# One row tile's normalisation moved to VectorE, key streams in another order, and an epsilon on VectorE, in a four-layer attention and MLP kernel

## The chip, the core and the metric

The kernel runs on one core of a Trainium2 chip. Its engines work side by side and wait for one another through semaphores: TensorE (matrix products, PE in the profile, with PEld for its weight loads), VectorE (DVE), ScalarE (ACT), GpSimd (POOL) and SyncE (SP), which here only issues DMAs. The metric is the device time of one execution in microseconds. Before the change it is 742.9 us, the median of three runs (742.76 to 743.25).

## The reference

An input x of 2048 rows (tokens) by 576 features passes through four layers, each with a residual: attention A, MLP B, then A and B again with the same weights.

```
x = x + A(layernorm(x));  x = x + B(layernorm(x));  x = x + A(layernorm(x));  x = x + B(layernorm(x))

A(x):  q, k, v = x @ wqkv            # 32 heads of 18 features
       phi(t) = where(t > 0, t + 1, exp(t)) + 1e-6
       kv = phi(k)^T v  per head;  z = sum over rows of phi(k)
       o = (phi(q) kv) / (phi(q) . z + 1e-6);   return o @ wo
B(x):  h = gelu(layernorm(x) @ w1 + b1)         # 4608 hidden features
       return h @ w2 + b2
```

The attention is linear: keys and values of all rows are first summed to one small matrix per head, and only then are the queries used. The denominators get 1e-6 added before the division.

## The kernel before

**Tiles.** The 2048 rows are 16 row tiles of 128 partitions, in four blocks of four tiles. x_sb holds x row by row, yT the normalised rows transposed (feature by row), as TensorE wants them. TensorE accumulates in eight PSUM banks: four single ones named one0 to one3 and two pairs, accA and accB. Program order on each engine is written out by hand: every engine executes in the order in which the code issues, and waits only for semaphores.

**Row tiling.** Most products use 64 of the 128 rows of TensorE's array, so that two streams, an upper (rows 0 to 63) and a lower one, run at the same time. A result is the sum of both halves, so both streams write the same PSUM bank in turn. Where one stream takes a bank over from the other, a relay stands between them: a tiny memset on GpSimd (`relay_by_pool`, line 306; in the MLP a copy on ScalarE) that waits for the last product of the one stream, and that the first product of the other stream waits for.

**The second attention's key stage.** `key_rows` (line 736) writes two lists of products, `upper` and `lower` (lines 813 to 818): `keys(t, hi)` are the key and value projections of tile t, nine products into two banks in turn of one0 to one2; `main(t, hi, k)` are the products of normalised rows with phi(k), into four banks k = 0 to 3 (accA, accB); `sides` are small products into one3. `row_streams` (line 261) merges the lists with a small planner: each product costs its columns at 2.4 per ns, a bank passes from stream to stream `PASS` = 0.5 us after its last product, and the stream that is ready first issues. Then it places relays: for each pass of a bank from product x to product y it looks for an existing relay between them that is due `RELAY` = 0.7 us before y, and else sets one as late as that allows. One relay may serve several banks, and then it waits for the last of its products. `key_half` (line 763) reads a finished bank: exponential and maximum with zero on ScalarE, sums on VectorE. That frees the bank for a later tile.

**The run-up to an MLP's first block.** After the key sums come the output products of the first block's tiles in the order 0, 2, 1, 3 (`wo_stage`), each followed on VectorE by the residual into x_sb and the statistics of the next layer's normalisation. `first` (line 1066) lists the four normalisations `Norm(t, "B", eng, transpose)`: `eng` says which engine normalises the row, `transpose` which one copies the transposed tile from PSUM to yT. Before, ScalarE normalises and copies the tiles 0 and 2, VectorE the tiles 1 and 3. GpSimd computes the reciprocal root (`rstd`, line 419: ln_u, ln_rstd, and ln_nmr where ScalarE normalises). Two query projections (`q_next`) go to one0 and one3, and ScalarE evicts them (an exponential and a maximum each). Then TensorE transposes tiles 0 and 2 (`transposed_halves`, line 469), and runs `q_batch` (line 671): 36 products for four query groups of the last block, into one2, one0, one1 and one3. The dictionary `between` names the number of products after which the transposes of tiles 1 and 3 come in. The MLP's first products (`m1_group`) follow.

**The denominators** of blocks 1 to 3 are computed within the MLP's first groups: `den_stage((1, 2, 3))` (line 971) sums them in one bank, ScalarE adds 1e-6 in place with an Identity activation whose bias is the constant tile den_eps, and VectorE takes the reciprocals. These go through DRAM to be spread over the partitions (`spread`), VectorE scales the queries with them, and `wo_pair` uses those.

Of the kernel before, what the change touches and what calls it, by code (L numbers as in the profile page):

```python
# [7 lines left out]
ACT = mybir.ActivationFunctionType  # L8
ALU = mybir.AluOpType
BF16 = mybir.dt.bfloat16  # L10
F32 = mybir.dt.float32
# [4 lines left out]
P = 128  # L16
NT = S // P
KD = 5
# [17 lines left out]
def build(tc, A_x, A_wqkv, A_wo, B_w1, B_b1, B_w2, B_b2, out, n_layers=4):  # L36
    nc = tc.nc
    with ExitStack() as ctx:
# [70 lines left out]
        quad_mask = const.tile([P, 4, P], BF16, name="quad_mask")  # L109
        zsel = const.tile([P, 6, H], BF16, name="zsel")  # L110
        eps_sel = const.tile([P, H], BF16, name="eps_sel")
        den_eps = const.tile([P, 1], F32, name="den_eps")
        last_two = const.tile([P, 2], F32, name="last_two")
        zk = const.tile([P, P], BF16, name="zk")

        def mask_batches():
            sel, fill = pool.affine_select, pool.memset
# [11 lines left out]
            def maskz_b():  # L129
                first = fill(zsel[:], 0.0)  # L130
                fill(eps_sel[:], 1e-6)
                fill(den_eps[:], 1e-6)
                fill(zk[:], 0.0)
                fill(last_two[:], 0.0)
                sel(out=last_two[:], in_=last_two[:], compare_op=ALU.not_equal, fill=1.0,
                    base=-126, pattern=[[-1, 2]], channel_multiplier=1)
                return first
# [123 lines left out]
        def row_streams(upper, lower, relay):  # L261


            ends, left, order, free, latest = [0.0, 0.0], [list(upper), list(lower)], [], {}, 0.0
            while left[0] or left[1]:
                ready = [max([ends[hi], latest] + [t + PASS for other, t in free.get(left[hi][0].bank, {}).items() if other != hi])
                         if left[hi] else 1e9 for hi in range(2)]
                hi = 0 if ready[0] <= ready[1] else 1
                op = left[hi].pop(0)
                op.at = latest = ready[hi]  # L270
                ends[hi] = op.at + max(op.n, 100) / 2400.0
                free.setdefault(op.bank, {})[hi] = ends[hi]
                order.append(op)

            user, passes = {}, []
            for i, op in enumerate(order):
                if op.bank in user and order[user[op.bank]].hi != op.hi:
                    passes.append((user[op.bank], i))
                user[op.bank] = i
            relays, needs = {}, {}  # L280
            for x, y in sorted(passes, key=lambda p: p[1]):
                found = [i for i in relays if x <= i < y and order[i].at + RELAY <= order[y].at]
                if not found:
                    found = [max([i for i in range(x, y) if order[i].at + RELAY <= order[y].at] or [x])]
                relays.setdefault(found[0], set()).add(x)
                needs.setdefault(y, set()).add(found[0])
            done, passed = {}, {}
            for i, op in enumerate(order):
                done[i] = op.emit()
                for r in needs.get(i, ()):  # L290
                    tc.add_manual_dep(done[i].ins, passed[r], SYNC, reason="row tiles take turns on a PSUM bank")
                if i in relays:
                    by = relay()
                    for x in relays[i]:
                        tc.add_manual_dep(by.ins, done[x].ins.name, SYNC, reason="row tiles take turns on a PSUM bank")
                    passed[i] = by.ins.name
                if op.then is not None:
                    op.then()


        PASS, RELAY = 0.5, 0.7

        def relay_by_act():
            return act.copy(out=relay_sb[:, 1:2], in_=relay_sb[:, 0:1])
# [257 lines left out]
        def layer_A(li, next_kind, begin, before_tile, before_keys, mid_tile, rows_ahead, after_tile, q_tiles, placed, mlp):  # L562
# [173 lines left out]
            def key_rows():  # L736
# [53 lines left out]
                def sides(t, hi):  # L790
                    rows, ops = HALVES[hi], []
                    for g in range(4):
                        def emit(g=g):
                            if "side" not in acc:
                                acc["side"] = one("side_ps", "one3")
                            first = "s" not in begun
                            begun.add("s")
                            return mm(acc["side"][:, 65 * g:65 * (g + 1)], pks[t][rows, GO[g]:GO[g] + P], ys[t][rows, 4 * P:D + 1],
                                      first, False, skip_group_check=True)
                        ops.append(RowOp("s", hi, 65, emit))  # L800
                    ops.append(RowOp("s", hi, 72, lambda: mm(acc["side"][0:VW, 264:336], vas[t][rows, :], pks[t][rows, V4:D],
                                                             False, False, skip_group_check=True)))
                    return ops

                def all_of(t, hi):
                    s = sides(t, hi)
                    return [main(t, hi, 0), main(t, hi, 1), main(t, hi, 2), s[0], main(t, hi, 3)] + s[1:]

                def some(t, hi, *ks):
                    return [main(t, hi, k) for k in ks]  # L810

                acc["main"] = [pair("rk_ps", "accA"), pair("rk_ps", "accB")]
                upper = some(0, 0, 0, 1) + keys(2, 0) + some(0, 0, 2, 3) + sides(0, 0) + keys(3, 0) + all_of(1, 0)
                lower = some(0, 1, 2, 3) + some(1, 1, 2, 3) + some(0, 1, 0, 1) + some(1, 1, 0, 1) + keys(2, 1) + sides(0, 1) + \
                    sides(1, 1) + keys(3, 1)
                for t in range(4, NT):
# [154 lines left out]
            def den_stage(cs):  # L971

                dp = one("den_ps", "one3" if cs[0] == 0 else None)
                for i, c in enumerate(cs):
                    to = dp[:, i * P:(i + 1) * P]
                    dens[c] = to
                    for g in range(G):
                        for j in range(TPC):
                            mm(to[32 * j:32 * (j + 1), :], zsel[:, g + (g == 4 and j // 2), :], q_tile(g, c, j),
                               g == 0 and i == 0, g == G - 1 and c > 0, skip_group_check=True)  # L980
                if cs[0] == 0:
                    for j in range(TPC):
                        mm(dp[32 * j:32 * (j + 1), 0:P], eps_sel[:], ident[:], False, True, skip_group_check=True)
                    return
                these = dp[:, 0:len(cs) * P]
                act.activation(out=these, in_=these, func=ACT.Identity, bias=den_eps[:, 0:1], scale=1.0)

            dens = {}

# [73 lines left out]
                    vec.tensor_tensor(out=rows, in0=acc[:, 0:HALF], in1=rows, op=ALU.add)  # L1063


            first = [Norm(t, "B", "act" if i < 2 else "dve", "act" if i < 2 else "dve") for i, t in enumerate((0, 2, 1, 3))]

            if not placed:
                most_sums()
# [56 lines left out]
            for tag in ("one0", "one3"):  # L1126
# [4 lines left out]
            first[0].transposed_halves(other[0])  # L1131
            first[1].transposed_halves(other[1])
            q_batch([units[:, i, :] for i in range(13, 17)], ("one2", "one0", "one1", "one3"),
                    {13: lambda: first[2].transposed_halves(other[0]), 25: lambda: first[3].transposed_halves(other[1])})
            one_turn.update(n=0, banks=4)
            warm_table(ACT.Gelu_apprx_tanh)
            assert not q_left
# [338 lines left out]
```

## Time and profile before

| what | value |
|---|---|
| median of three runs | 742.9 us |
| the profiled execution | 743.14 us |
| its span in the trace | 741.3 us |
| TensorE busy | 735.1 us, 99% |
| ScalarE busy | 302.7 us, 41% |
| VectorE busy | 270.7 us, 37% |
| GpSimd busy | 132.4 us, 18% |
| granted TensorE clock | 1.0 |

A row of the timeline has the start in us, the duration, the engine, the line of the code, the operation, output and inputs by name with their shape, the number of merged instructions (x), and in brackets the engine's idle time before it and what ended that. L229 is the helper through which nearly all TensorE products are issued, L53 the one of the other engines, so rows are told apart by their tiles: q_ps, k_ps, rk_ps (the four main banks of the key stage), side_ps, den_ps, wo_ps, hp_ps and h_ps (first MLP product), m_ps (second MLP product), tp (transposes), y_ring (normalised rows), units (queries and hidden features), pool_relay (relays). In merged groups of products the duration runs from the first start to the last end, and ends are modelled, so a short wait can be hidden under the end of the product before it. The chain that ended last is a list of start, duration and what ran.

### The profile page before, as it was taken

The numbers are of one execution on the slowest core, as the hardware profiler recorded it, in microseconds if no ns is written. First come the engines' busy times: TensorE is split into PE (matmuls) and PEld (weight loads), VectorE is DVE, ScalarE is ACT, GpSimd is POOL, SyncE is SP. The second block draws the span as 40 slices with busy tenths as digits, with TensorE's granted clock in tenths as the row PEclk, the third lists the DMA queues.
The fourth block names the chain that finished last, engine by engine and source line by source line (L and its number), as shares of the span: only waits on it lengthen the run. The fifth ranks groups of instructions, "written<-read, shape, count | busy, mean of one in ns | idle before, by whom it ended". The sixth has DMA issues, their size and how long they took to land.

```text
span 741.3 us, 21145 instructions
## 1 busy us (share of the span) xinstructions
PE 735.1 (99%) x9142; PEld 468.6 (63%) x9151; DVE 270.7 (37%) x688; ACT 302.7 (41%) x672; POOL 132.4 (18%) x404
## 2 busy tenths in 40 slices
PE   8999999999999999999999999999999999999998
PEld 4666556774576457646777655667646754774475
DVE  7868745434224403300376685552410060000000
ACT  5776743107601750374035676320373047106700
POOL 4541000322121202200223120031200130010010
PEclk9999999999999999999999999999999999999999
DMA  8945221112200220110024000202020002000000
GB/s 204 267 145 186 70 71 35 22 34 53 36 5 31 37 37 18 29 26 2 18 74 94 23 8 24 82 2 54 18 37 2 18 17 37 10 18 10 1 17 18
DMA packets 61315, 35.02 MB, mean 47 GB/s; under 512 B 37126, under 2 KB 61222, under 8 KB 61222
## 3 DMA queue, kind: packets, MB, share of 16 engines
q1 hardware_dynamic: 60470, 33.45, 17.8%
q8 instruction: 71, 1.16, 0.7%
q10 hardware_dynamic: 752, 0.23, 0.2%
q14 instruction: 22, 0.18, 0.1%
HBM read 21.70 MB, written 4.93 MB: 36 GB/s over the span
## 4 chain that ended last, share of the span: by engine, by line
PE 95%; DVE 2%; ACT 1%; DMA 1%; SPq 1%; issue 0%; POOL 0%; DVEq 0%; POOLq 0%
PE m_ps L229 38%; PE hp_ps L229 21%; PE h_ps L229 17%; PE k_ps L229 5%; PE q_ps L229 4%; PE rk_ps L229 4%; PE wo_ps L229 4%; ACT units L53 1%; PE side_ps L229 1%; SPq L53 1%; DMA x_sb<-in_A_x_dram 1%; DVE units L53 1%; ACT y_ring L53 1%; PE tp L465 0%; DVE ln_st L53 0%; PE den_ps L229 0%
## 5 line engine op out<-in xcount | busy, mean ns | idle before, releaser
L229 PEld LDWEIGHTS <-units 64*128 64x128 bf16 (+1 forms) x5070 | 260.9, 94 | 72.8 <-DVE units L53 0.8
L229 PE MATMUL m_ps<-w_sb,units 64*128 64x288 bf16 (+2 forms) x4432 | 283.7, 283 | 0.0
L229 PEld LDWEIGHTS <-w_sb 64*128 64x128 bf16 x2304 | 126.8, 94 | 132.3 <-issue 0.7
L229 PE MATMUL h_ps<-yT,w_sb 64*128 64x512 bf16 x1152 | 176.3, 376 | 0.0
L229 PE MATMUL hp_ps<-yT,w_sb 64*128 64x512 bf16 x1152 | 149.7, 376 | 0.0
L53 DVE TENSOR_TENSOR x_sb<-m_ps,xo 128x288 bf16<-128x288 f32 (+3 forms) x48 | 25.4, 554 | 336.5 <-PE m_ps L229 336.5
L53 ACT COPY relay_sb<-relay_sb 128x1 f32<-128x1 f32 x142 | 27.1, 191 | 260.0 <-PE m_ps L229 176.3
L53 ACT ACTIVATE units<-hp_ps,b1T 128x512 bf16<-128x512 f32 x144 | 91.2, 684 | 87.0 <-PE hp_ps L229 87.0
L53 POOL TENSOR_TENSOR xo<-x_sb,b_bc 128x576 f32<-128x576 bf16 x32 | 40.8, 1275 | 345.1 <-DVE x_sb L53 319.8
L53 ACT ACTIVATE units<-h_ps,b1T 128x512 bf16<-128x512 f32 x142 | 95.2, 687 | 0.1
L229 PE MATMUL k_ps<-wkv_sb,yT 64*128 64x288 bf16 (+3 forms) x432 | 61.0, 299 | 0.3 <-ACT yT L53 0.2
L229 PE MATMUL hp_ps<-yT,w_tail 64*128 64x512 bf16 x144 | 54.1, 376 | 0.0
L229 PE MATMUL h_ps<-yT,w_tail 64*128 64x512 bf16 x144 | 54.1, 376 | 0.0
L53 DVE BATCH_NORM_STATS2 ln_st<-x_sb 128x6 f32<-128x288 bf16 x128 | 51.6, 443 | 1.5 <-DMA x_sb<-in_A_x_dram 0.8
L229 PE MATMUL q_ps<-yT,wq_sb 64*128 64x512 bf16 (+2 forms) x273 | 42.0, 347 | 1.1 <-ACT units L53 0.7
L53 DVE STREAM_TRANSPOSE shared<-y_ring 128x640 bf16<-128x640 bf16 x40 | 32.7, 832 | 26.0 <-DMA yT<-shared 19.9
L229 PEld LDWEIGHTS <-yT 64*128 64x128 bf16 (+1 forms) x448 | 36.4, 95 | 8.7 <-ACT yT L53 0.7
L229 PE MATMUL wo_ps<-shared,units 64*128 64x288 bf16 (+1 forms) x480 | 38.1, 283 | 0.2 <-DVE units L53 0.2
L53 ACT ACTIVATE phi_e<-k_ps 128x288 bf16<-128x288 f32 x64 | 26.3, 413 | 29.5 <-PE k_ps L229 25.9
L53 POOL MEMSET pool_relay<- 128x1 f32 x152 | 17.0, 112 | 118.1 <-PE hp_ps L229 44.1
L53 POOL TENSOR_TENSOR ln_rstd<-ln_u,neg_half 128x1 f32<-128x1 f32 x64 | 36.5, 571 | 8.4 <-DVE ln_u L53 3.3
L229 PEld LDWEIGHTS <-w_tail 64*128 64x128 bf16 x288 | 27.1, 94 | 17.0
(112 smaller groups left out, 493.8 us busy)
## 6 DMA issues: line engine op xcount, KB each, us to landing
yT<-shared SPq DMA_DIRECT2D x160, 40.0 KB
w_sb<-in_B_w_dram SPq DMA_DIRECT2D x12, 432.0 KB
w_sb<-in_B_w_dram SPq DMA_DIRECT2D x9, 512.0 KB
yT<-rden_rows SPq DMA_DIRECT2D x24, 126.0 KB
y_rows<-y_ring SPq DMA_DIRECT2D x16, 144.0 KB
units<-y_rows SPq DMA_DIRECT2D x16, 144.0 KB
x_sb<-in_A_x_dram SPq DMA_DIRECT2D x15, 144.0 KB
out_dram<-x_sb SPq DMA_DIRECT2D x15, 144.0 KB
```

The lines of the kernel that those rows point to most:

```text
L53: inst = issue(*args, **kw)
L229: return pe(nc.tensor.matmul(out_, lhsT=lhsT, rhs=rhs, start=start, stop=stop, **kw))
```

## The change

Four things change.

- The normalisation of tile 2, the second in `first`, is done by VectorE (`eng` "dve"); its transposed copy stays on ScalarE. In VectorE's order it stands after the statistics of the third tile and before the residual of the fourth. Both attention layers do so.
- The transposes of tiles 1 and 3 come after 17 and 26 products of the query batch, in place of 13 and 25.
- The 1e-6 of `den_stage` is added by VectorE, in place, and den_eps and its memset go. The first denominators, of block 0, are handled as before.
- In the second attention's key stage the upper list starts in another order: products of tile 1 are spread between those of tile 0 and the keys of tiles 2 and 3. And relays are placed by a new rule: within `SOON` = 0.25 us (in the planner's time) of the product that they wait for. GpSimd's stretch of relay memsets around this stage grows from 90 to 107.

```diff
-                found = [i for i in relays if x <= i < y and order[i].at + RELAY <= order[y].at]
-                if not found:
-                    found = [max([i for i in range(x, y) if order[i].at + RELAY <= order[y].at] or [x])]
+                soon = [i for i in range(x, y) if order[i].at <= order[x].at + SOON and order[i].at + RELAY <= order[y].at] or [x]
+                found = [i for i in relays if i in soon] or [max(soon)]
...
-        PASS, RELAY = 0.5, 0.7
+        PASS, RELAY, SOON = 0.5, 0.7, 0.25
...
-                upper = some(0, 0, 0, 1) + keys(2, 0) + some(0, 0, 2, 3) + sides(0, 0) + keys(3, 0) + all_of(1, 0)
+                third = keys(3, 0)
+                upper = some(0, 0, 0) + some(1, 0, 0) + some(0, 0, 1) + keys(2, 0) + some(0, 0, 2, 3) + sides(0, 0) + third[:KD] + \
+                    some(1, 0, 1) + third[KD:] + some(1, 0, 2, 3) + sides(1, 0)
...
-                act.activation(out=these, in_=these, func=ACT.Identity, bias=den_eps[:, 0:1], scale=1.0)
+                vec.tensor_scalar(out=these, in0=these, scalar1=1e-6, scalar2=None, op0=ALU.add)
...
-            first = [Norm(t, "B", "act" if i < 2 else "dve", "act" if i < 2 else "dve") for i, t in enumerate((0, 2, 1, 3))]
+            first = [Norm(t, "B", "act" if i < 1 else "dve", "act" if i < 2 else "dve") for i, t in enumerate((0, 2, 1, 3))]
...
-                    {13: lambda: first[2].transposed_halves(other[0]), 25: lambda: first[3].transposed_halves(other[1])})
+                    {17: lambda: first[2].transposed_halves(other[0]), 26: lambda: first[3].transposed_halves(other[1])})
```

More of the change, by code (lines that the diff above doesn't have):

```diff
@@ L111, in build @@
         eps_sel = const.tile([P, H], BF16, name="eps_sel")
-        den_eps = const.tile([P, 1], F32, name="den_eps")
         last_two = const.tile([P, 2], F32, name="last_two")
@@ L131, in maskz_b @@
                 fill(eps_sel[:], 1e-6)
-                fill(den_eps[:], 1e-6)
                 fill(zk[:], 0.0)
```

## The prediction

> **What bounds the kernel now.** I read the page first (busy shares, the chain that ended last), then the timeline of the two stretches that the change touches, engine by engine, then the waits of the key stage.
>
> ```profile
> span 741.3 us, 21145 instructions
> ...
> PE 95%; DVE 2%; ACT 1%; DMA 1%; SPq 1%; issue 0%; POOL 0%; DVEq 0%; POOLq 0%
> ```
>
> TensorE carries 95% of the chain that ended last, and its instructions are almost the same before and after (the change reorders 179 of some 18,300 TensorE instructions and adds none). So only the moments in which TensorE waits can be won or lost. The change touches three such places: the run-up to each MLP's first block (twice), the denominators (twice), and the key stage of the second attention (once).
>
> **First place: the run-up to the first block.** ScalarE, then TensorE, around 72 to 80 us:
>
> ```profile
> 72.09 1.08 ACT L53 ACTIVATE units<-q_ps 128x512 bf16<-128x512 f32 x2
> 73.06 0.87 ACT L53 ACTIVATE y_ring<-x_sb,ln_nmr,ln_rstd 128x576 bf16<-128x576 bf16 x1
> 73.95 0.24 ACT L53 COPY y_ring<-y_ring 128x64 bf16<-128x64 bf16 x1
> 74.11 2.06 ACT L53 ACTIVATE units<-q_ps 128x512 bf16<-128x512 f32 x4
> 76.03 1.31 ACT L53 COPY yT<-tp 128x640 bf16<-128x640 bf16 x2
> ```
>
> ```profile
> 74.33 0.47 PE L476 MATMUL tp<-ident,y_ring 64*128 64x64 bf16 x20
> 74.63 1.24 PE L229 MATMUL q_ps<-yT,wq_sb 64*128 64x512 bf16 x9
> 76.21 0.61 PE L229 MATMUL q_ps<-yT,wq_sb 64*128 64x512 bf16 x4 [0.34 <-ACT units L53]
> 76.79 0.32 PE L476 MATMUL tp<-ident,y_ring 64*128 64x64 bf16 x10
> ...
> 79.45 0.38 PE L229 MATMUL hp_ps<-yT,w_sb 64*128 64x512 bf16 x1
> ```
>
> ```profile
> 439.08 0.61 PE L229 MATMUL q_ps<-yT,wq_sb 64*128 64x512 bf16 x4 [0.34 <-ACT units L53]
> ```
>
> Nine products of the query batch start from 74.63; the group lasts 1.24 and one product about 0.38, so eight spacings are 0.86 and one is 0.108. The tenth was due at 74.63 + 9 x 0.108 = 75.60 and came at 76.21: 0.61 us lost (the page shows 0.34 of it as idle, the rest lies under the modelled end of the ninth). It waited for the last of the four ScalarE evictions that end at 74.11 + 2.06 = 76.17, and these had stood behind tile 2's normalisation and its padding copy, from 73.06 to 74.11. The second layer's row, 363 us later, has the same wait.
>
> The change takes that pair (1.05 us of ScalarE's queue) to VectorE. *ScalarE's side:* its evictions may now start as their products end.
>
> ```profile
> 72.07 2.32 PE L229 MATMUL q_ps<-yT,wq_sb 128*128 128x512 bf16 x10
> ```
>
> The last of these ten products ends at 72.07 + 2.32 = 74.39; its pair of evictions then runs from some 74.4 for half of 2.06, to 75.45, and the batch's tenth product can go at about 75.5. It is also due then: the ten are (2.32 - 0.38) / 9 = 0.216 apart, so the transposes could start at 74.23, 0.1 sooner, had tile 2's padding copy not ended at 74.19 only. 76.21 becomes 75.5: 0.7 us. From there 27 products of 0.108 and two sets of ten transposes (0.14 each, 76.79 to the next product at 76.93) give 3.2 us: the first MLP product at about 78.72 instead of 79.45.
>
> *VectorE's side* decides whether that holds. These are VectorE and GpSimd:
>
> ```profile
> 74.58 0.21 DVE L53 BATCH_NORM_AGGREGATE ln_mv<-ln_st 128x2 f32<-128x12 f32 x1
> 74.71 0.38 DVE L53 TENSOR_SCALAR y_ring<-x_sb,ln_mv,ln_rstd 128x576 bf16<-128x576 bf16 x1
> 75.12 0.18 DVE L53 COPY y_ring<-y_ring 128x64 bf16<-128x64 bf16 x1
> 75.81 0.43 DVE L53 TENSOR_SCALAR y_ring<-x_sb,ln_mv,ln_rstd 128x576 bf16<-128x576 bf16 x1 [0.50 <-POOL ln_rstd L53]
> 76.27 0.18 DVE L53 COPY y_ring<-y_ring 128x64 bf16<-128x64 bf16 x1
> 76.36 0.29 DVE L53 TENSOR_SCALAR units<-units 128x512 bf16<-128x512 bf16 x1
> 76.68 0.43 DVE L53 TENSOR_TENSOR units<-units 128x512 bf16<-128x512 bf16 x1
> 77.15 0.49 DVE L53 COPY yT<-tp 128x640 bf16<-128x640 bf16 x1
> 78.59 0.49 DVE L53 COPY yT<-tp 128x640 bf16<-128x640 bf16 x1 [0.95 <-PE tp L476]
> ```
>
> ```profile
> 74.88 0.26 POOL L53 TENSOR_SCALAR ln_u<-ln_mv 128x1 f32<-128x1 f32 x1 [0.90 <-DVE ln_mv L53]
> 75.22 0.55 POOL L53 TENSOR_TENSOR ln_rstd<-ln_u,neg_half 128x1 f32<-128x1 f32 x1
> ```
>
> A normalisation and its padding copy cost VectorE 0.41 (74.71 to 75.12) and about 0.1 more to the next start (76.27 to 76.36): 0.51 us. They go ahead of tile 3's residual and statistics, so the aggregate moves from 74.58 to 75.09; GpSimd's two steps and the last normalisation follow, each 0.51 later: 75.81 becomes 76.32, the query sum 76.87, the first copy into yT 77.66, the second 78.18 and its end 78.67. The first MLP product reads all four tiles, so it starts at about 78.75: VectorE and TensorE arrive within 0.05 us of each other. The 0.95 us that VectorE idled before its second copy is used up: it is the cover that hides the added work, and what is late next. The gain is 79.45 - 78.75 = 0.70. The bounds: were the pair as long on VectorE as on ScalarE (1.05), the start would be 79.29 and the gain 0.16; nothing lets it exceed TensorE's 0.73. I take 0.68, since VectorE's own rows price the pair.
>
> The transposes of tiles 1 and 3 move from the 13th and 25th to the 17th and 26th product, that is to about 76.4 and 77.5. By then tile 1's row (about 75.9), tile 3's (77.0) and the two PSUM pairs (ScalarE's copies, 76.03 to 77.34 before, 0.6 sooner now) are there, so the move costs nothing; at 13 it would wait on VectorE's later row for tile 1. GpSimd loses one small step per layer (the mean's product, needed only for ScalarE's form), on no path.
>
> **Second place: 1e-6 by VectorE.**
>
> ```profile
> 92.59 0.56 ACT L53 ACTIVATE den_ps<-den_ps,den_eps 128x384 f32<-128x384 f32 x1
> ```
>
> ```profile
> 93.18 1.77 DVE L53 RECIPROCAL rden<-den_ps 128x128 bf16<-128x128 f32 x2 [3.31 <-ACT den_ps L53]
> ```
>
> ```profile
> 105.20 0.29 PE L229 MATMUL wo_ps<-shared,units 64*128 64x288 bf16 x1 [0.24 <-DVE units L53]
> ```
>
> ```profile
> 467.23 4.60 PE wo_ps L229 x71
> ```
>
> ```profile
> 475.71 4.41 PE wo_ps L229 x72
> ```
>
> The chain reciprocal, two rounds of DMA, scaling ends in a wait of TensorE: 0.24 us idle in the first MLP, and in the second 4.60 against 4.41 for the same work undisturbed, 0.19. Whatever VectorE saves ahead of the first reciprocal is saved there, up to these waits. VectorE has been idle for 3.31 us, so nothing stands in its queue. The nearest VectorE row for 384 float32 columns of PSUM is the one below, four of 512 columns in 2.48 us, 0.62 each, so at most 0.62 and in proportion 0.47:
>
> ```profile
> 79.44 2.48 DVE L53 TENSOR_SCALAR units<-q_ps 128x512 bf16<-128x512 f32 x4 [0.35 <-ACT units L53]
> ```
>
> ScalarE's 0.56 plus the hand-over (93.18 - 93.15 = 0.03) against 0.47 to 0.62: between 0.12 won and 0.03 lost, per layer. I take 0.07. ScalarE's freed 0.56 us serves gelu evictions that TensorE does not wait for. The memset of den_eps that goes, 0.1 us of GpSimd early in the program, is on no path.
>
> **Third place: the key stage of the second attention** (382 to 414.8 us), where two row streams of TensorE hand PSUM banks to each other through a GpSimd memset.
>
> ```profile
> 382.50 0.09 PEld L229 LDWEIGHTS <-units 64*128 64x128 bf16 x1 [0.25 <-issue]
> ```
>
> ```profile
> 385.24 0.09 PEld L229 LDWEIGHTS <-pk 64*128 64x128 bf16 x1 [0.36 <-POOL pool_relay L53]
> ```
>
> ```profile
> 384.79 0.40 ACT L53 ACTIVATE pk<-k_ps 128x288 bf16<-128x288 f32 x1
> ```
>
> ```profile
> PEld L229 <- POOL pool_relay L53: 1.0, 4, 0.4
> ```
>
> ```profile
> L53 POOL MEMSET pool_relay<- x88: 98/99/220, 382.4 to 413.9; 128x1 f32 x88
> ```
>
> Two early stalls are of PSUM banks, not of relays. At 382.50 tile 2's keys start late, behind a query eviction; the weight loads stood 0.25, of which about 0.13 is loss, since the products before are 0.21 apart. At 385.24 tile 3's second half waits for the bank of tile 2's first half, whose last reader ends at 384.79 + 0.40 = 385.19; 0.36 in the row, and the hint at the relay is the last semaphore only. The new order puts a product of tile 1 ahead of each, 0.21 us of other work, so it can win 0.13 + 0.21 = 0.34. Part comes back: the next bank is given up by ScalarE and VectorE, which run no faster, and the new order makes the lower stream wait for the upper one's second product on its first bank. The remaining waits of the 1.0 (about 0.6 in three) are relays on the side bank; the "soon" rule gives each hand-over its own, earlier memset (107 in GpSimd's stretch instead of 90), which helps only where a memset waited for a product of another bank. At worst the 0.34 becomes its own negative; at best it holds and half of the 0.6 goes. Range from 0.64 won to 0.34 lost; I take 0.17 won, half of the early stalls, since their rows are the nearest and their giving back is only partly seen.
>
> **The lock.** In this stage a memset lasts 99 ns in the median and 220 at most: a VectorE operation runs beside the long ones. The Trainium skill, "SBUF — State Buffer", section "Who interferes with whom", gives a rule for that: a VectorE tensor_scalar or copy in a two-port mode and a GpSimd operation exclude each other, whoever comes second waits for the whole instruction. By that rule the longest memset, 121 ns over the median, agrees, and the rule speaks against this change twice: 17 more memsets to be caught, and two more such VectorE operations beside GpSimd's rstd steps. In the run-up GpSimd's step at 74.88 already took 0.26 beside VectorE's 0.38, and the shift above carries that length along.
>
> **The sum.** 2 x 0.68 + 2 x 0.07 + 0.17 = 1.67 us. The profiled execution took 743.14 us (span 741.3 and 1.84 around it), 0.24 above the median of 742.9. So 741.47 on its own scale and 741.2 on the median's: 0.2% less. From no change, a measurement of this kernel tells about 0.2%, 1.5 us, so the forecast lies just past that line.
>
> **Rivals.**
> *VectorE becomes the bound.* Its queue has no idle time left, and each tenth that the pair costs over 0.51 delays the first product by a tenth. At 1.05 the first place gives 0.16 per layer, total 2 x 0.16 + 0.14 + 0.17 = 0.63: 742.3. For it: the two arrivals within 0.05 us. Against: VectorE's own rows for just this pair.
> *The wait only changes its owner.* TensorE's tenth product finds another thing late (the PSUM pair of tile 3's residual, now 0.51 us later on VectorE, under the second ten transposes), and the first place gives nothing: 0.31 in all, 742.6. Against is the residual's row:
>
> ```profile
> 73.00 0.70 DVE L53 TENSOR_TENSOR x_sb<-wo_ps,x_sb 128x576 bf16<-128x576 f32 x1
> ```
>
> It moves to 73.51 and ends at 74.21, and the second ten transposes want it at about 74.4.
> *Slower: relays caught by VectorE.* A stretched memset delays its product by up to 0.12 us; 14 tiles pass through the stage, and with two close hand-overs in each this is 14 x 2 x 0.12 = 3.4 us. With the other places' 1.5 won it gives 744.8. It decides above 3.0 / 14 = 0.21 us per tile, that is when both hand-overs of nearly every tile are hit. Before, only a few were, as the median of 99 shows; the steady pattern of products is not changed by the new start, which speaks against it.
>
> **How the numbers follow.** Forecast 0.65, VectorE as the bound 0.15, changed owner 0.10, caught relays 0.10. The forecast's own range is 740.8 to 741.8: the first place 0.55 to 0.72 per layer, the second -0.03 to 0.12, and the third's ends half reached. It falls below 741.41 (faster by over 0.2%) in 0.50 of all and within 0.2% in 0.15. The next two cases are within: 0.40 in all. Slower by over 0.2%: 0.10. The range from 740.8 to 742.6 takes in the first two rivals and leaves out the caught relays and the forecast's edges.
>
> **What would show it.** Right: no ScalarE normalisation before the four evictions, which end near 75.5; the tenth product without a wait; the first MLP product 0.6 to 0.7 us sooner after the output products; the same again 363 us later; no long idle of VectorE ahead of its second copy; VectorE's addition near 0.5 us and the scaling 0.07 sooner; no wait at the starts of tile 2's and tile 3's keys, and a key stage within 0.3 us of before. Wrong: VectorE's second copy ending more than 0.1 us after the last query product; memsets of 0.2 us in every tile of the key stage, with tiles longer than before; a new wait at the transposes.

## The result, and the profile after

The changed kernel takes 741.31 us, the median of 13 runs (741.11 to 741.59), against 742.93 us (742.59 to 743.80, 13 runs) for the kernel before: 1.62 us less, a ratio of 0.9978 with a 95% interval of 0.9970 to 0.9987. That is just past the 0.2% that a measurement of this kernel tells from no change. The profiled execution took 741.47 us, its span 739.7.

The page of the kernel after: its head, and the first line of the chain that ended last.

```profile
span 739.7 us, 21185 instructions
...
PE 97%; DVE 1%; DMA 1%; SPq 0%; issue 0%; POOL 0%; DVEq 0%
```

TensorE's share of the chain went from 95% to 97%: TensorE does the same work and waits less. L227, L474 and L463 are the lines that were L229, L476 and L465 before.

**First place.** The timeline of the kernel after around 73 us, ScalarE and then TensorE:

```profile
73.21 2.16 ACT L53 ACTIVATE units<-q_ps 128x512 bf16<-128x512 f32 x4 [0.20 <-PE q_ps L227]
75.26 1.30 ACT L53 COPY yT<-tp 128x640 bf16<-128x640 bf16 x2
```

```profile
74.18 0.47 PE L474 MATMUL tp<-ident,y_ring 64*128 64x64 bf16 x20
74.48 2.10 PE L227 MATMUL q_ps<-yT,wq_sb 64*128 64x512 bf16 x17
...
78.59 0.38 PE L227 MATMUL q_ps<-yT,units 64*128 64x512 bf16 x1
78.71 1.12 PE L227 MATMUL hp_ps<-yT,w_sb 64*128 64x512 bf16 x8
...
436.67 2.10 PE L227 MATMUL q_ps<-yT,wq_sb 64*128 64x512 bf16 x17
```

No normalisation stands ahead of the four evictions, which end at 75.37. The query batch runs 17 products without a break, in the second layer too (the last row), and the first MLP product starts at 78.71. VectorE, in the same view:

```profile
72.84 0.38 DVE L53 TENSOR_SCALAR y_ring<-x_sb,ln_mv,ln_rstd 128x576 bf16<-128x576 bf16 x1
73.25 0.18 DVE L53 COPY y_ring<-y_ring 128x64 bf16<-128x64 bf16 x1
73.35 0.75 DVE L53 TENSOR_TENSOR x_sb<-wo_ps,x_sb 128x576 bf16<-128x576 f32 x1
...
76.20 0.43 DVE L53 TENSOR_SCALAR y_ring<-x_sb,ln_mv,ln_rstd 128x576 bf16<-128x576 bf16 x1 [0.50 <-POOL pool_relay L53]
...
77.92 0.49 DVE L53 COPY yT<-tp 128x640 bf16<-128x640 bf16 x1
78.41 2.48 DVE L53 TENSOR_SCALAR units<-q_ps 128x512 bf16<-128x512 f32 x4
```

The pair costs VectorE 0.51 (72.84 to 73.35), and the second copy into yT has no idle time left ahead of it. (The row at 76.20 names pool_relay, the semaphore event nearest in time; by its inputs it waits for ln_rstd, as before.)

**Second place.** VectorE around the denominators, and the wait that the saving should have met:

```profile
91.70 0.57 DVE L53 TENSOR_SCALAR den_ps<-den_ps 128x384 f32<-128x384 f32 x1 [2.85 <-PE den_ps L227]
92.30 1.77 DVE L53 RECIPROCAL rden<-den_ps 128x128 bf16<-128x128 f32 x2
```

```profile
104.44 0.29 PE L227 MATMUL wo_ps<-shared,units 64*128 64x288 bf16 x1 [0.36 <-DVE units L53]
```

The addition takes 0.57 us, as long as ScalarE's 0.56, and the hand-over to the reciprocal is still 0.03. TensorE's wait is no shorter.

**Third place.** The waits of the key stage (381 to 416 us) and its group of relays:

```profile
PEld L227 <- issue: 0.5, 2, 0.3
PEld L227 <- POOL pool_relay L53: 0.2, 1, 0.2
```

```profile
L53 POOL MEMSET pool_relay<- x105: 98/98/195, 381.9 to 413.1; 128x1 f32 x105
```

TensorE's waits put down to relays fell from 1.0 us in four to 0.2 in one, and a new one of 0.22 (put down to "issue") stands at 386.59. One might expect more than half a microsecond from that. The stage as a whole says otherwise.

**Where the time went.** The best ruler here is the first product of each kind on TensorE. The table cuts the span at such starts, read from the timeline of each kernel (us). The run-up goes from the first kv_ps product (the small key-value matrix) to the first hp_ps one; the key stage from the first rk_ps product of the second attention to its first kv_ps one, 381.95 to 420.44 before and 381.19 to 419.61 after.

| kernel | start to kv_ps | run-up 1 | to den_ps | to wo_ps | to m_ps | key stage | run-up 2 | to den_ps | to wo_ps | to m_ps |
|---|---|---|---|---|---|---|---|---|---|---|
| before | 57.60 | 21.85 | 12.01 | 12.64 | 25.50 | 38.49 | 21.89 | 12.00 | 12.62 | 25.19 |
| after | 57.45 | 21.26 | 11.84 | 12.66 | 25.63 | 38.42 | 21.29 | 11.84 | 12.62 | 25.06 |
| before_again | 57.74 | 21.85 | 12.01 | 12.65 | 26.01 | 38.49 | 21.87 | 12.00 | 12.62 | 25.04 |
| after_again | 57.61 | 21.26 | 11.84 | 12.67 | 25.42 | 38.41 | 21.29 | 11.84 | 12.62 | 25.05 |
| norm_move | 57.99 | 21.26 | 11.84 | 12.64 | 25.49 | 38.65 | 21.29 | 11.84 | 12.62 | 25.24 |
| norm_old_places | 57.48 | 21.22 | 12.01 | 12.63 | 25.48 | 38.65 | 21.25 | 12.00 | 12.62 | 25.24 |
| den_alone | 57.86 | 21.86 | 12.00 | 12.67 | 25.47 | 38.66 | 21.88 | 12.01 | 12.63 | 25.21 |
| den_plus1 | 57.46 | 21.85 | 12.01 | 12.66 | 25.47 | 38.49 | 21.87 | 12.01 | 12.62 | 25.19 |
| keys_both | 57.35 | 21.86 | 12.01 | 12.64 | 25.58 | 38.76 | 21.88 | 12.01 | 12.62 | 25.34 |
| after_plus2 | 57.35 | 21.26 | 11.84 | 12.66 | 25.50 | 38.76 | 21.29 | 11.84 | 12.62 | 25.06 |
| after_plus4 | 57.31 | 21.26 | 11.84 | 12.66 | 25.47 | 38.49 | 21.30 | 11.84 | 12.62 | 25.06 |
| norm_twice | 57.36 | 21.75 | 11.84 | 12.67 | 25.46 | 38.41 | 21.79 | 11.84 | 12.98 | 25.06 |

The first two rows tell the result: 0.59 and 0.60 us in the two run-ups, 0.17 and 0.16 more up to the den_ps products, nothing from there to wo_ps (12.64 to 12.66, 12.62 both), 0.07 in the key stage. That is 1.59 us. The start of the program (57.31 to 57.99 over all kernels, none of which changes anything there that TensorE waits for) and the stretch to the first m_ps, which holds the denominators' round trip through DRAM (25.50 and 26.01 in the kernel before alone), differ from execution to execution and prove nothing.

The rows after the first two are of the experiments.

### The profile page after: what moved, and what is told of

Same layout as the page of the kernel before. It is cut to its first block, busy times and chain, and to the rows that moved or that the text cites. A ratio compares the mean times of both kernels' runs of the same rounds, so it can differ in the third digit from the quotient of the medians.

```text
span 739.7 us, 21185 instructions
## 1 busy us (share of the span) xinstructions
PE 734.7 (99%) x9151; PEld 526.8 (71%) x9151; DVE 272.6 (37%) x694; ACT 300.0 (41%) x666; POOL 132.2 (18%) x418
## 3 DMA queue, kind: packets, MB, share of 16 engines
q8 instruction: 71, 1.16, 0.7%
## 4 chain that ended last, share of the span: by engine, by line
PE 97%; DVE 1%; DMA 1%; SPq 0%; issue 0%; POOL 0%; DVEq 0%
PE m_ps L227 38%; PE hp_ps L227 20%; PE h_ps L227 17%; PE q_ps L227 5%; PE k_ps L227 5%; PE wo_ps L227 5%; PE rk_ps L227 4%; PE side_ps L227 1%; PE tp L463 0%; DVE ln_st L53 0%; PE den_ps L227 0%; PE kvwo_ps L227 0%; PE kv_ps L227 0%; DMA x_sb<-in_A_x_dram 0%; PE rden_ps L227 0%; DMA yT<-rden_rows 0%
## 5 line engine op out<-in xcount | busy, mean ns | idle before, releaser
L227 PEld LDWEIGHTS <-units 64*128 64x128 bf16 (+1 forms) x5070 | 289.1, 94 | 44.7 <-DVE units L53 0.7
L227 PE MATMUL m_ps<-w_sb,units 64*128 64x288 bf16 (+2 forms) x4432 | 283.8, 283 | 0.0
L227 PEld LDWEIGHTS <-w_sb 64*128 64x128 bf16 x2304 | 148.4, 94 | 107.2 <-DVE rden L53 0.7
L227 PE MATMUL h_ps<-yT,w_sb 64*128 64x512 bf16 x1152 | 172.9, 376 | 0.0
L227 PE MATMUL hp_ps<-yT,w_sb 64*128 64x512 bf16 x1152 | 152.6, 376 | 0.0
L227 PE MATMUL k_ps<-wkv_sb,yT 64*128 64x288 bf16 (+3 forms) x432 | 60.7, 299 | 0.2
L227 PE MATMUL hp_ps<-yT,w_tail 64*128 64x512 bf16 x144 | 54.2, 376 | 0.0
L227 PE MATMUL h_ps<-yT,w_tail 64*128 64x512 bf16 x144 | 54.2, 376 | 0.0
L227 PEld LDWEIGHTS <-yT 64*128 64x128 bf16 (+1 forms) x448 | 36.3, 95 | 8.9 <-ACT yT L53 0.7
L227 PE MATMUL q_ps<-yT,wq_sb 64*128 64x512 bf16 (+2 forms) x282 | 42.1, 348 | 0.0
L227 PE MATMUL wo_ps<-shared,units 64*128 64x288 bf16 (+1 forms) x480 | 38.1, 283 | 0.4 <-DVE units L53 0.4
L53 DVE TENSOR_SCALAR y_ring<-x_sb,ln_mv,ln_rstd 128x576 bf16<-128x576 bf16 (+2 forms) x62 | 29.1, 476 | 23.7 <-POOL ln_rstd L53 22.9
```

The costliest lines, as they stand in the source:

```text
L53: inst = issue(*args, **kw)
L227: return pe(nc.tensor.matmul(out_, lhsT=lhsT, rhs=rhs, start=start, stop=stop, **kw))
```

## The experiments

### The parts one by one

*norm_move*: the kernel before with the normalisation and the places of the transposes.

```
+ first = [Norm(t, "B", "act" if i < 1 else "dve", ...
+         {17: lambda: first[2]..., 26: lambda: first[3]...})
```

> The kernel before with tile 2's normalisation on VectorE and the transposes after 17 and 26 products, nothing else. Theory (the prediction's first place): 0.68 us per layer, 1.36 us in all, so a ratio near 0.9982 and a median near 741.55; the tenth query product of the batch without a wait, twice. Rival (the trace of after is read wrongly, and the second block's 0.84 us comes from the key stage or the denominators): 0.6 us per layer in the first block only and less than 1.0 us in all, a median above 741.9.

Measured: 742.03 us against 743.06 of the kernel before on the same chip, ratio 0.9985 (0.9976 to 0.9994). The run-ups and the stretches to den_ps are those of the whole change to the hundredth, in both layers. So the second block's gain is the first place again, and the rival falls by the trace. The median alone would not have decided it: it gains 1.03, not 1.36, and lies on the rival's side of 741.9. One reason is seen in the table: the key stage, whose code is untouched, takes 0.16 us longer than before.

*norm_old_places*: the same with the transposes still after 13 and 25 products.

> Tile 2's normalisation on VectorE, but the transposes of tiles 1 and 3 still after 13 and 25 products. Theory: tile 1's row ends at 75.70 and its PSUM pair is read by 76.0, while the thirteenth product starts at about 75.9; so the old places cost 0 to 0.1 us per layer and the median is within 0.3 us of the kernel with the new places. Rival (the move is a needed half of the change): the transposes wait for VectorE's later row, 0.3 us or more per layer, and the kernel is 0.6 us or more slower than the one with the new places.

Measured: 741.91 us, ratio 0.9985 (0.9976 to 0.9994). The median is no worse than norm_move's. The table shows the two ways apart: the first MLP product is 0.04 sooner with the old places, the den_ps products 0.13 later (21.22 + 12.01 against 21.26 + 11.84). What differs is the order of TensorE's products at the change-over. With the old places:

```profile
77.84 1.04 PE L229 MATMUL q_ps<-yT,wq_sb 64*128 64x512 bf16 x8
78.70 0.38 PE L229 MATMUL hp_ps<-yT,w_sb 64*128 64x512 bf16 x1
78.72 0.38 PE L229 MATMUL q_ps<-yT,units 64*128 64x512 bf16 x1
78.92 0.83 PE L229 MATMUL hp_ps<-yT,w_sb 64*128 64x512 bf16 x6
```

One row stream has its last query product only after the other has begun the MLP, as in the kernel before (79.45 and 79.47 there). With the new places the last query product comes first (78.59, then 78.71). That this order is what costs the 0.13 is read from the rows and was not tried by itself. Whatever the cause, the first MLP product is a marker that is about a tenth too early in the old order, and the gain of the first place is better read at den_ps: 0.76 per layer with the new places, 0.63 with the old. The transposes did not have to wait at their old places.

*den_alone*: only the addition of 1e-6 by VectorE.

```
- fill(den_eps[:], 1e-6)
...
- act.activation(out=these, in_=these, func=ACT.Identity, bias=den_eps[:, 0:1], scale=1.0)
+ vec.tensor_scalar(out=these, in0=these, scalar1=1e-6, scalar2=None, op0=ALU.add)
```

> Only the 1e-6 by VectorE. The prediction's step: the reciprocals 0.07 us sooner per layer, 0.14 us in all, 742.8. The row of after (0.57 us on VectorE against 0.56 on ScalarE, with a hand-over of about 0.03 on either side): nothing, 742.9 with an uncertainty of 0.2, and the wait ahead of the output products as long as before. Rival (ScalarE is what benefits: its queue loses 0.56 us among the gelu evictions): the h_ps products after the den sums start 0.15 us sooner, and the total falls by 0.3 us.

Measured: 743.34 us, ratio 1.0003 (0.9995 to 1.0012). From den_ps to wo_ps 12.67 and 12.63, against 12.64 and 12.62: nothing won, and ScalarE's free time reaches nobody either, since the rival's h_ps products lie in the same stretch. Again the untouched key stage is longer, 38.66.

*keys_both*: only the new order and the relay rule.

> Only the key stage: the new order and the relay rule. The prediction: 0.17 us won (between 0.64 won and 0.34 lost). The trace of after: from the first attention's end to the second's key sums 0.07 us won beside the 0.76 of the first block, so 742.85, the same within the uncertainty. Rival (the whole of the second block's larger gain, 0.84 against 0.60, was the key stage's doing through another phase of GpSimd's relays): 0.3 us won, 742.6.

Measured: 743.38 us, ratio 1.0004 (0.9996 to 1.0013). The stage takes 38.76, while the same code in the changed kernel takes 38.42. The parts' medians add up to -1.03 + 0.28 + 0.32 = -0.43 us, the whole is -1.62. Of the missing 1.2 us, 0.67 lie in the key stage: each part alone lengthens it (0.16, 0.17, 0.27), all together shorten it (0.07). The rest was not traced; it is less than the 0.7 us to either side that the interval of one such median leaves open.

### Does the stage repeat?

*after_again* and *before_again* are the two kernels once more, on one chip.

> The changed kernel once more, on the same chip as the three below. Theory A (the key stage falls into one of several patterns of relays, set by how its start lies to GpSimd and VectorE, so that equal code takes between 38.4 and 38.8 us there): the key stage, from its first main product to the second attention's kv_ps, need not be the 38.42 of the first trace; the places outside it repeat within 0.05: 21.26 from the first kv_ps to the first MLP product, 21.29 in the second layer. Theory B (the stage's time is fixed by the code around it): 38.42 again within 0.03. Median 741.3 to 741.9.

> The kernel before once more, for its trace. Theory A: the key stage is 38.65, as in the three kernels that left it alone, or 38.49 as in the first trace, by chance of the start. Theory B: 38.49 again. Outside it nothing moves by over 0.05 us but the start of the program (57.4 to 58.0 us to the first kv_ps). Ratio 1.000 within 0.0008.

Measured: 741.44 against 743.11, ratio 0.9976 (0.9966 to 0.9986), and 743.10, ratio 0.9999 (0.9990 to 1.0008). The key stage takes 38.41 and 38.49, as in the first traces. So it is no chance of the start (theory A falls): the time belongs to the program, and yet it depends on code far away.

### What far-away code changes

The kernels differ ahead of the key stage in the number of GpSimd's instructions. Against the kernel before, den_alone lacks one memset (den_eps), norm_move one small step of the first layer (the mean's product that only ScalarE's form needs) and keys_both none; the whole change lacks both. I numbered GpSimd's records, waits included, in order of time. Start in us after the stage's first rk_ps product, and in brackets the time since the record ahead:

```
den_alone   323 wait for PE  7.327 (0.696)   324 memset       7.700 (0.373)
den_plus1   324 wait for PE  7.325 (0.693)   325 memset       7.409 (0.084)
keys_both   323 memset       5.902 (0.084)   324 wait for PE  6.197 (0.295)
after       322 wait for PE  6.034 (0.129)   323 memset       6.118 (0.084)   324 wait for PE  6.413 (0.295)
```

Most memsets of the stage follow their wait by 0.084 us, and none of the others by more than 0.25; where the memset is record 324 (or 452) it is 0.373. Over all traces of this case the records 196, 324, 452 and 580 stand out, 128 apart: the shortest time since the record ahead is 0.229 us at these numbers, and at any other place of the cycle of 128 it is 0.084 or less. Record 68, one step earlier, does not stand out: it came 0.04 us after the one ahead in five of the fourteen traces. The page of every kernel here has instruction DMAs in blocks (the columns are packets, megabytes and share), these after:

```profile
q8 instruction: 71, 1.16, 0.7%
...
q14 instruction: 22, 0.18, 0.1%
```

0.18 MB in 22 packets are 8 KB each. The 1.16 MB of queue 8, spread over TensorE's 18,302 products and weight loads, are about 64 bytes for one, and at that size, by estimate, 8 KB are 128 instructions. That the pause is the step from one block of instructions to the next is inferred from this equality; that the pause exists, and where, is measured.

The traces leave this inference open. VectorE, ScalarE, GpSimd and SyncE have 2,846 records together in this trace, and 22 packets of 128 are 2,816, so queue 14 seems to serve all four; yet VectorE and ScalarE show no such pause. A packet of the queue starts 2.8 to 3.6 us behind record 324 in every trace, but in eight of the fourteen none starts within 18 us behind record 580. And no run tells a pause in the instructions from one in the profiler's recording of them. By the Trainium skill, "Runtime: NRT & Kernel Launch", section "Instruction fetch mechanics", the sequencer streams its instructions through a DMA queue of its own in blocks of 256, and crossing a block is mostly hidden; TensorE's packets of 16 KB agree with that, while for GpSimd the period is 128 records, and the pause shows unless the record at the boundary is itself a wait that lasts longer. In den_alone it is record 323, the one ahead, that waits long; record 324 is the memset behind it, and the pause is paid in full.

To test what the pause does to the stage, spare memsets at the start of the program shift the numbers and do nothing else:

```
+ for i in range(k):
+     fill(spare[:, i:i + 1], 0.0)
```

*den_plus1*: den_alone with one.

> The 1e-6 by VectorE alone, as in the run before, but with one spare GpSimd memset at the start of the program in place of den_eps's, so that GpSimd's records in the key stage have the numbers of the kernel before again. Theory (every 128th record of GpSimd, numbers 324 and 452 here, comes no sooner than about 0.3 us after the one ahead of it; with one instruction fewer that falls on a relay's memset in place of a wait): record 324 is a wait again, the memset of 0.36 us delay is gone, the key stage is 38.49 in place of 38.66. Rival (VectorE's addition itself, 290 us earlier, changed the stage's phase): 38.66 again.

Measured: 742.97 us against 742.99, ratio 1.0001 (0.9993 to 1.0010), and the stage is back at 38.49. The timelines of TensorE, den_alone first (the spare lines make L227 L230):

```profile
382.21 0.65 PE L227 MATMUL rk_ps<-pk,units 64*128 64x504 bf16 x4
...
420.87 0.33 PE L227 MATMUL kv_ps<-shared,wkv_sb 128*126 128x126 bf16 x3
```

```profile
381.80 0.65 PE L230 MATMUL rk_ps<-pk,units 64*128 64x504 bf16 x4
...
420.29 0.39 PE L230 MATMUL kv_ps<-shared,wkv_sb 128*126 128x126 bf16 x4
```

One idle memset 380 us earlier makes the stage 0.17 us shorter. In GpSimd's timeline the late record is seen as a longer idle time ahead of the relay, den_alone and then den_plus1:

```profile
389.91 0.26 POOL L53 MEMSET pool_relay<- 128x1 f32 x2 [0.88 <-PE k_ps L227]
```

```profile
389.20 0.33 POOL L53 MEMSET pool_relay<- 128x1 f32 x2 [0.59 <-PE side_ps L230]
```

0.88 in place of 0.59, which is the 0.29. The name of the releaser is only that of the semaphore event nearest in time.

*after_plus2*: the changed kernel with two, so that the numbers are those of keys_both.

> The changed kernel with two spare GpSimd memsets at the start of the program. Theory: the numbers of GpSimd's records in the key stage are those of the kernel with the key change alone, so the stage takes 38.76 as there, in place of 38.42, and the median is 0.35 us above the changed kernel's, at about 741.7. Rival (the other parts of the change are what shortened the stage by 0.35 against the key change alone): 38.42 again and 741.4.

Measured: 741.77 us against 742.99, ratio 0.9984 (0.9975 to 0.9993); the stage takes 38.76, as in keys_both to the hundredth, and its longest memset, 0.259 us, is again that of keys_both:

```profile
L53 POOL MEMSET pool_relay<- x105: 98/98/259, 381.7 to 413.2; 128x1 f32 x105
```

So the other parts of the change do not help the key stage by what they do; they took two instructions out of GpSimd's stream, and that moved the pause from the relay that it hits in keys_both to a later one.

*after_plus4*: with four, so that both pauses fall where GpSimd waits for long anyway.

> The changed kernel with four spare GpSimd memsets. Theory: record 324 is then the wait ahead of which GpSimd idles 0.99 us in the trace of after (now record 320), and 452 one ahead of which it idles 0.49 (now 448), so neither costs anything; the changed kernel's own record 324 came 0.295 after the one ahead, 0.13 late by the trace of the key change alone. The stage takes 38.1 to 38.3, and the median falls by 0.1 to 0.3 us to 741.1 to 741.3. Rival: 38.42 again.

Measured: 741.46 us, ratio 0.9979 (0.9970 to 0.9987), 0.31 below after_plus2 on the same chip, where the stages differ by 0.27; the intervals of the two medians overlap, so it is the stage that shows it. These two kernels have the same tiles and differ in two memsets alone, so the place of the tiles in SBUF is not what sets the stage's time. The records fell as planned (324 came 0.989 after the one ahead, 452 0.494), but the stage takes 38.49, 0.07 more than in the changed kernel. My expectation was wrong: a pause less is not time less. Perhaps each pause also shifts which later relay meets a VectorE operation and which does not; that was not tried. I can say from a trace where a pause lies, not what the stage will take without it.

### Relays held up by VectorE

*one_sum*: the kernel before, with minimum and sum of phi in one instruction in the key stage, since the two-step form's first step stretched the memsets beside it.

```
- vec.tensor_scalar(out=e, in0=e, scalar1=1.0, scalar2=1e-6, op0=ALU.min, op1=ALU.add)
- vec.tensor_tensor(out=dst, in0=dst, in1=e, op=ALU.add)
+ vec.scalar_tensor_tensor(out=dst, in0=e, scalar=1.0, in1=dst, op0=ALU.min, op1=ALU.add)
```

> The kernel before, with the two VectorE steps of phi (minimum and 1e-6, then the sum) made one scalar_tensor_tensor for the queries and the first key halves of the second attention's key stage; it leaves out the 1e-6 of phi there. Theory (VectorE's tensor_scalar on bf16 holds GpSimd's memsets up): no memset that begins under such a step is left, the memsets over 0.135 us fall from 15 or 16 to a third, and the stage is 0.2 to 0.4 us shorter. Rival (the memsets are stretched by something else, or the late relays follow from TensorE's own order): as many long memsets and the stage within 0.1 us of 38.5 to 38.65.

Measured: 743.15 us against 743.11, ratio 1.0000 (0.9991 to 1.0009), the stage 38.52. Only part of the edit took: the first key halves are single instructions now, but the three query sums that fall into the stage come from another helper and kept their tensor_scalar, as the second key halves were meant to. VectorE's groups in the stage:

```profile
L53 DVE SCALAR_TENSOR_TENSOR pk<-phi_e,pk 128x288 bf16<-128x288 bf16 x14 | 6.4, 459 | 11.2 <-ACT pk L53 11.2
...
L53 DVE TENSOR_SCALAR units<-units 128x512 bf16<-128x512 bf16 x3 | 0.9, 285 | 0.0
```

The memsets over 0.135 us fell from 16 to 6, three of these beside the query sums and three beside the second key halves. So it is this form of VectorE's instruction, on bfloat16 tiles, that stretches them. Over all traces a memset that starts later than 0.07 us into such a tensor_scalar ends 0.035 to 0.039 us after it (here one of 0.212 ends at 388.727, the tensor_scalar beside it at 388.690), and one that starts in its first 0.06 us keeps its 0.098. In this run one that starts during a scalar_tensor_tensor, or during the tensor_scalar that reads q_ps in float32, lasts 0.098 to 0.099. That agrees with the Trainium skill, "SBUF — State Buffer", section "Who interferes with whom". But ten stretched relays gone won nothing. Whether the six that are left cost anything was not tried.

*one_sum_after*: the same edit on the changed kernel.

> The same edit on the changed kernel. Theory: the changed order and relay rule are as good as the planner has them (its plan is 0.4 us longer than the old one's) and only lack of collisions made it shorter, so 38.2 to 38.4 in the stage and 741.0 to 741.3 us in all. Rival (the query sum, now longer in one piece, delays the banks): slower than the changed kernel by 0.2 us or more.

Measured: 741.74 us against 743.11, ratio 0.9981 (0.9972 to 0.9989), the stage 38.37. 0.05 us off the stage, nothing that the median shows. There was little to take away: the changed kernel has 8 memsets over 0.135 us, this one 7. Neither this edit nor the spare memsets beat the changed kernel.

### What is late next

*norm_twice*: the changed kernel, tile 2's pair done twice on VectorE.

```
  if t == 2:
      first[1].norm()
+     vec.tensor_scalar(out=n.y[:, 0:D], in0=x_sb[:, n.t, :], scalar1=n.mv[:, 0:1], scalar2=n.r, ...)
+     vec.tensor_copy(out=n.y[:, D:DPAD], in_=n.y[:, 4 * P:D])
```

> The changed kernel with tile 2's normalisation and padding copy on VectorE done twice, 0.51 us more of its queue ahead of the first block of each MLP. If VectorE were the bound there, as the prediction's first rival and its 0.05 us of slack have it: 0.46 to 0.51 us per layer, 0.9 to 1.0 in all. By the trace of after VectorE's last copy ends at 78.42 and the first MLP product starts at 78.71: 0.26 us of slack, so 0.25 per layer and 0.5 us in all, with TensorE waiting ahead of hp_ps for VectorE's yT copy.

Measured: 742.69 us against 742.99, ratio 0.9995 (0.9986 to 1.0004): 1.3 us slower than the changed kernel, each taken against the kernel before on its own chip. The run-ups grow by 0.49 and 0.50, and from den_ps to wo_ps the second layer pays 0.36 more, whose cause stays open. The size is that of VectorE as the bound, but the place is not. TensorE and VectorE of norm_twice:

```profile
74.09 0.32 PE L474 MATMUL tp<-ident,y_ring 64*128 64x64 bf16 x10
74.74 0.32 PE L474 MATMUL tp<-ident,y_ring 64*128 64x64 bf16 x10 [0.33 <-DVE x_sb L53]
...
79.11 1.12 PE L227 MATMUL hp_ps<-yT,w_sb 64*128 64x512 bf16 x8
```

```profile
73.38 0.43 DVE L53 TENSOR_SCALAR y_ring<-x_sb,ln_mv,ln_rstd 128x576 bf16<-128x576 bf16 x1
73.84 0.18 DVE L53 COPY y_ring<-y_ring 128x64 bf16<-128x64 bf16 x1
73.94 0.75 DVE L53 TENSOR_TENSOR x_sb<-wo_ps,x_sb 128x576 bf16<-128x576 f32 x1
...
78.02 0.88 DVE L53 COPY yT<-tp 128x640 bf16<-128x640 bf16 x2
```

The copies into yT end at 78.02 + 0.88 = 78.90, 0.21 ahead of the first MLP product. The wait is at the second ten transposes, whose PSUM bank tile 3's residual has to empty: it ends at 73.94 + 0.75 = 74.69, the transposes start at 74.74. Counted from kv_ps, the residual came 0.68 later than in the changed kernel (73.94 - 57.36 = 16.58 against 73.35 - 57.45 = 15.90) and TensorE lost 0.49, so the changed kernel has 0.19 us of slack there. (The expectation's 0.26 at the copy is 0.29 by the two times that it names.)

## Why the prediction was right, point by point

It gave 741.2 us, the median is 741.31; its gain of 1.67 stands beside 1.62. The total is right, its terms less so: the first was too small by 0.16 us over both layers, the other two too large by 0.24 together. That these nearly cancel is luck.

- **First place, 0.68 per layer: right mechanism, right place, measured 0.76 at den_ps.** The evictions end at 75.37 (said 75.45), the tenth product has no wait, and the second layer repeats the first. Of the 0.76, the normalisation's move is 0.63, by norm_old_places; the other 0.13 came with the transposes' new places, which the prediction put at nothing while it held 0.73 for the most that could be won. At the first MLP product, the marker I named, the gain is 0.59 and 0.60: in the old order that product ran ahead of the last query product, so it is an early marker there.
- **VectorE's side.** The pair's 0.51 is exact. Its arrival was taken as within 0.05 of TensorE's; in the trace its last copy ends at 78.41, 0.30 ahead of the first MLP product. What is really late next is tile 3's residual, the thing the second rival named, 0.19 us away, so the first tenths that the pair costs over 0.51 would not all have been paid.
- **"The move costs nothing."** It even wins: 0.13 per layer at den_ps, by the traces of norm_move and norm_old_places, though their medians do not show it. The reason given for it, that at the 13th product a transpose would wait for VectorE's row, did not show: no wait stands there with the old places.
- **Second place, 0.07 per layer: mis-sized, it is 0.** VectorE takes 0.57 us for the 384 columns, at the upper part of the range of 0.47 to 0.62. The value in proportion to columns was the wrong one to take; the row's whole 0.62 was nearer.
- **Third place, 0.17: measured 0.07, and for another reason.** The two early stalls did go, as said, and one of 0.22 came. But the stage's time in this program is 38.42 where GpSimd's pauses fall well and 38.76 where they fall badly, with the same products and relays. The step that failed is the one that priced the stage by its own waits alone. With the changed order and relay rule but GpSimd's old record numbers the stage is 0.27 longer than before (keys_both), so even the sign of this term was luck. The term's range (0.64 won to 0.34 lost) held both.
- **The removed instructions.** The memset of den_eps and the mean's product were said to be on no path. As work they are not. As places in GpSimd's stream they moved the key stage: den_alone lost 0.17 there for one memset, and den_plus1 won it back.
- **Rivals.** VectorE as the bound by the copies: no, though a pair more would make VectorE the bound at the residual. Changed owner: not reached, by 0.19 us. Caught relays: some are, 0.195 us at the longest in the changed kernel, but not in every tile. The passage on the lock expected more of them, for 17 more memsets; there are fewer, 8 over 0.135 us among 105 against 16 among 88, and in the kernel before ten fewer of them won nothing.

## What to carry to other kernels

Where one engine carries the chain, price a change by the moments in which that engine waits, and look for the next late thing among all that share the queue which got the work: here not the last copy but a PSUM bank two steps earlier. Where parts measured alone do not add up to the whole, compare starts of the same product from kernel to kernel over the whole span: the difference may lie in code that no part touches. An effect of 0.2 to 0.4 us in a stage of close hand-overs is not a property of the edit until a do-nothing instruction has been shown not to cause it.

## What the runs showed of the hardware that I had not expected

- Every 128th record of GpSimd from 196 on (196, 324, 452, 580; 68 does not) comes 0.229 us or more after the one ahead, 0.295 to 0.373 at most relays, where most others follow within 0.084. Why is open. Where the record is itself a longer wait nothing is seen of it; on a relay it moved a 38.5 us stage by 0.17 us (one spare memset) and 0.34 us (two). No such step was seen for VectorE or ScalarE, whose shortest distances stay under 0.1 at every place of the cycle.
- A GpSimd memset of 0.098 us that starts later than 0.07 us into a VectorE tensor_scalar on bfloat16 tiles ends 0.035 to 0.039 us after it, 0.26 us long at the most in these traces.
- The stage's time is the same to 0.01 us in two executions of one program, while the stretch with a round trip through DRAM differs by 0.5 us (25.50 and 26.01 in the kernel before).
- An in-place VectorE addition over 128x384 float32 in PSUM takes 0.57 us, ScalarE 0.56.
